# The experts' items of 128 tokens in float32 instead of split float32r, in an attention, expert and feed-forward kernel

## The chip, the core and the metric

The kernel runs on one core of a Trainium2 chip. A core has a matrix engine (TensorE, PE in the profile; its weight loads are PEld), a vector engine (VectorE, DVE), an engine for activations (ScalarE, ACT), GpSimd (POOL) and SyncE (SP), which here issues nearly all DMAs. They work side by side and wait for each other by semaphores. Operands lie in SBUF, and TensorE writes its sums to PSUM. The metric is the time of one execution on the device in microseconds (us), as the median of several runs.

## The reference

Three layers follow one another. The middle one is touched by the change: tokens that pass a skip score go to one of eight experts each, the one with the largest logit.

```python
def _moe_ref(x, w_skip, w_gate, w1, w2):      # x [4608 or fewer rows of 4352, 512], w1 [8, 512, 1024], w2 [8, 1024, 512]
    ...                                        # do_compute, e_idx, gate_w from x @ w_skip and x @ w_gate
    for e in range(E):
        mask = e_idx == e
        h = np.maximum(xc[mask] @ w1[e], 0.0)
        y[mask] = gate_w[mask, None] * (h @ w2[e])
    out[do_compute] = xc + y
```

Before it stands a two-way attention with 8 blocks of 512 + 32 rows, behind it a feed-forward layer over all 4352 rows with weights of 512 x 2048 and 2048 x 512. All arrays are float32, except those last weights, which come as float64.

## The kernel before

The program has three stages: the attention, which also routes the tokens (each token's row, its gate and its number go to a scratch array `xs`, sorted by expert); the experts (class `Experts`, method `run`); and the feed-forward layer (`ffn`, which takes up two thirds of the time).

The experts work through items. An item of 512 tokens is handled by `first` or `item_a`, one of 128 tokens by `item_b`. How many there are depends on the data; the trace shows one `first`, four rounds of the loop over `item_a` (L1037) and four of the loop over `item_b` (L1041). In these loops the item after the present one is loaded ahead: its weights come in eight DMAs of 512 KB on SP's queue, four with parts of w1 (`fetch1`, L711) into the buffers `two1` (seen by parts as `raw1`) and four with parts of w2 (`fetch2`, L717) into `two2` (`raw2`). The last round loads the weights of an item that does not exist, which nobody reads.

TensorE multiplies in float32r, a reduced form of float32. To keep the accuracy, every operand is a sum of two float32r tiles: `split` (L766 to L769) casts the raw tile on ACT (the high part) and subtracts it from the raw one on DVE or POOL (the low part). A product is then three matmuls (`PAIRS`: high x high, high x low, low x high).

An item of 128 tokens runs as follows. The rows `xb` are copied to `xc` (L983), and SP fetches the next item's rows into `xb` (L984) and its w1 (L711). Eight splits bring raw w2 to `w2p` (`split2`, the odd ones with POOL for the subtraction), each followed, after every second one, by the fetch of the next item's part of w2. `s1(0)` and `s1(1)` multiply the turned rows `xTb` by `w1p`: 24 matmuls of 512 columns (L993), and ACT applies the ReLU (L998). Then three turns by `trx` (L773 to L776: four transposes of 128 x 128 on TensorE and a split of the result): `hs[0]`, the next item's rows `xb`, `hs[1]`. `s2` multiplies the turned h by `w2p`: 24 matmuls of 512 columns (L1007); beside them the next item's w1, which has arrived, is split (`split1`). `gated` (L902) adds the result to the item's rows, `take_wait` (L906) lets POOL wait for it, and `scatter` (L732) stores the rows. The turns share two PSUM buffers (tag "tr"), so that the third has to wait until the first one's result has been split. Each engine runs its instructions in this order, and goes into the next round of the loop without a wait for the other engines.

At the end of a loop SP waits until the stores and fetches of the loop have landed (the waits of L1041), and the engines meet before the feed-forward layer begins with `fetch` of rows (L1178) and conversions of its weights (L1115 and further).

## Time and profile before

| | |
|---|---|
| median of 3 runs | 1239.1 us (1238.55 to 1243.37) |
| the profiled execution | 1242.4 us span; no time of its own around the span is given |
| TensorE busy, share of the span | 95% |
| VectorE, ScalarE, GpSimd busy | 47%, 38%, 19% |
| the rounds of `item_b`, from L993's first dense matmul to the last of L1007 | 385.88 to 459.65 us of the span |
| the first work of the feed-forward layer | 465.4 us |

Times within a trace are microseconds from the start of the span. A busy TensorE is not a TensorE at its peak: its records overlap, so the time from one start to the next (the pitch) tells its rate, not the length of a record. The granted clock (PEclk) is 1.00 at 2.4 GHz and 0.50 at 1.2 GHz; a value between is a mean over a window.

### The profile page before, as it was taken

What the parts mean: (1) busy time and instruction counts of PE and PEld (TensorE: products, weight loads), DVE (VectorE), ACT (ScalarE), POOL (GpSimd) and SP (SyncE); (2) the same over time, 40 slices, a digit from 0 to 9 for tenths busy, and PEclk for the clock granted to TensorE, in tenths of its full rate; (3) what the DMA queues carried; (4) which work ended last, traced back from release to release, by engine and by line L of the source; (5) the groups of instructions that cost most, each with busy time, mean ns of one, the idle gap of its engine ahead of it and who ended that gap; (6) DMA issues with size and microseconds to landing.
All of it is one profiled execution on the core that took longest, in us unless ns stands there. A gap on an engine that the chain in (4) does not pass through costs nothing.

```text
span 1242.4 us, 16595 instructions
## 1 busy us (share of the span) xinstructions
PE 1177.9 (95%) x5916; PEld 952.0 (77%) x5916; DVE 579.4 (47%) x993; ACT 470.2 (38%) x866; POOL 237.9 (19%) x241
## 2 busy tenths in 40 slices
PE   7898989999997768999999999999999999999998
PEld 4666767888886556888888888888888888888886
DVE  6878684535435877777432232322322322232222
ACT  7775354334335545444422222222322322222222
POOL 4666341101104545555100000000000000000000
PEclk9899989999998888999999999999999999999999
DMA  6866674524525755332210000000000000000000
GB/s 190 282 227 211 232 238 161 176 94 135 184 87 178 250 204 188 102 103 68 69 35 17 26 26 17 34 17 18 35 18 17 34 17 17 34 1 1 34 1 34
DMA packets 76048, 118.42 MB, mean 95 GB/s; under 512 B 11344, under 2 KB 48208, under 8 KB 75216
## 3 DMA queue, kind: packets, MB, share of 16 engines
q1 hardware_dynamic: 71344, 106.00, 25.7%
q0 software_dynamic: 4640, 11.57, 2.5%
q8 instruction: 40, 0.66, 0.2%
q14 instruction: 24, 0.20, 0.0%
HBM read 84.74 MB, written 36.49 MB: 98 GB/s over the span
## 4 chain that ended last, share of the span: by engine, by line
PE 52%; DVE 6%; ACT 2%; issue 2%; DMA 0%; POOL 0%; SPq 0%; DVEq 0%; ACTq 0%; POOLq 0%
PE po L1244 25%; PE ph L1224 25%; DVE gg L1231 1%; DVE cv L1122 1%; ACT g L1233 1%; PE ptx L1205 1%; DVE cv L1115 1%; DVE cv L1126 1%; DVE g L1234 1%; DVE cv L1131 1%; ACT gg L1230 1%; ACT W L1137 0%; DMA xw<-x_in_dram 0%; ACT W L1118 0%; DVE xt L1213 0%
## 5 line engine op out<-in xcount | busy, mean ns | idle before, releaser
L1244 PE MATMUL po<-W,g 128*128 128x512 f32 x1632 | 393.5, 389 | 0.0
L1224 PE MATMUL ph<-xt,W 128*128 128x512 f32 (+1 forms) x1536 | 352.5, 378 | 5.5 <-DVE gg L1231 3.3
L1244 PEld LDWEIGHTS po<-W,g 128*128 128x128 f32 x1632 | 305.3, 188 | 62.7
L1224 PEld LDWEIGHTS ph<-xt,W 128*128 128x128 f32 x1536 | 275.1, 188 | 61.2 <-DVE gg L1231 5.5
L1231 DVE SCALAR_TENSOR_TENSOR gg<-gg,ph 128x512 f32<-128x512 f32 (+1 forms) x144 | 94.8, 658 | 356.9 <-ACT gg L1230 356.9
L1230 ACT ACTIVATE gg<-ph,three 128x512 f32<-128x512 f32 (+1 forms) x144 | 95.7, 665 | 346.8 <-PE ph L1224 342.0
L1234 DVE TENSOR_TENSOR g<-gg,g 128x512 fp32r<-128x512 f32 (+1 forms) x144 | 98.9, 687 | 95.5 <-ACT g L1233 95.5
L1233 ACT CAST g<-gg 128x512 fp32r<-128x512 f32 (+1 forms) x144 | 86.1, 598 | 129.8 <-DVE gg L1231 129.8
L854 PE MATMUL ph<-xTa,w1p 128*128 128x512 f32 x480 | 120.7, 402 | 5.9 <-DVE w1p L769 4.3
L866 PE MATMUL po<-w2p,hT 128*128 128x512 f32 x480 | 120.5, 398 | 0.0
L854 PEld LDWEIGHTS ph<-xTa,w1p 128*128 128x128 f32 x480 | 91.9, 192 | 28.0 <-DVE w1p L769 4.7
L866 PEld LDWEIGHTS po<-w2p,hT 128*128 128x128 f32 x480 | 89.6, 189 | 20.1
L859 DVE SCALAR_TENSOR_TENSOR hT<-ph,hT 128x512 fp32r<-128x512 f32 x40 | 27.6, 691 | 94.3 <-ACT hT L858 91.2
L858 ACT ACTIVATE hT<-ph 128x512 fp32r<-128x512 f32 x40 | 23.9, 599 | 121.0 <-PE ph L854 121.0
L769 DVE TENSOR_TENSOR w1p<-raw,w1p 128x512 fp32r<-128x512 f32 x72 | 56.2, 805 | 9.2 <-ACT w1p L768 8.2
L769 DVE TENSOR_TENSOR w2p<-raw,w2p 128x512 fp32r<-128x512 f32 x56 | 53.7, 972 | 4.7 <-PE ph L993 4.4
L277 PE MATMUL pxr<-BD,AT 128*128 128x265 f32 x128 | 41.9, 450 | 5.0 <-ACT XR L281 1.8
L768 ACT CAST w1p<-raw 128x512 fp32r<-128x512 f32 x80 | 45.8, 620 | 2.1 <-DMA raw<-in_moe_w_dram 2.1
L1224 PE MATMUL ph<-raw,W 128*128 128x512 f32 x192 | 46.6, 391 | 0.0
L906 POOL TENSOR_TENSOR seen<-xr 128x1 f32<-128x1 f32 x24 | 8.4, 352 | 196.7 <-DVE xr L902 154.2
L1138 POOL TENSOR_TENSOR W<-cv,W 128x512 fp32r<-128x512 f32 x32 | 43.8, 1385 | 10.8 <-ACT W L1137 10.7
L768 ACT CAST w2p<-raw 128x512 fp32r<-128x512 f32 x72 | 42.3, 619 | 3.5 <-DVEq L1037 1.7
(216 smaller groups left out, 1055.3 us busy)
## 6 DMA issues: line engine op xcount, KB each, us to landing
raw<-in_moe_w_dram SPq DMA_DIRECT2D x80, 512.0 KB, 6.5
raw<-in_moe_w_in_dram SPq DMA_DIRECT2D x16, 512.0 KB
raw<-in_moe_w_out_dram SPq DMA_DIRECT2D x16, 512.0 KB
x_in_dram<-XR SPq DMA_DIRECT2D x8, 1024.0 KB
xw<-x_in_dram SPq DMA_DIRECT2D x14, 512.0 KB
out_dram<-raw SPq DMA_DIRECT2D x13, 512.0 KB
xn<-xs_dram SPq DMA_DIRECT2D x6, 1028.0 KB, 5.8
X<-in_x_dram SPq DMA_DIRECT2D x6, 1024.0 KB
```

Source lines behind the costliest of these rows:

```text
L277: nc.tensor.matmul(px, lhsT=AT[b, q][:, P * c:P * c + P], rhs=BD[:, 2 * b + q, :], start=True, stop=True,)
L768: nc.scalar.copy(hi, src)
L769: (eng or nc.vector).tensor_tensor(lo, src, hi.bitcast(F32), op=ALU.subtract)
L854: nc.tensor.matmul(ph, lhsT=w1p[a][:, f, kk, :], rhs=xTa[b][:, kk, :], start=(n == 0), stop=(n == 11))
L866: nc.tensor.matmul(po[c], lhsT=hp[f][a][:, P * c:P * c + P], rhs=w2p[b][:, f, :], start=(f == 0 and n == 0), stop=(f == NF - 1 and n == 2),)
L1138: nc.gpsimd.tensor_tensor(lo[i], a[i], hi[i].bitcast(F32), op=ALU.subtract)
L1224: nc.tensor.matmul(ph[:, :n], lhsT=W1[f][a][:, kk, :], rhs=xt[j][b][kk // 2][:, kk % 2, :n], start=(i == 0), stop=(i == 11),)
L1230: nc.scalar.activation(gg[:, :n], ph[:, :n], AF.Relu, bias=k["three"])
L1231: nc.vector.scalar_tensor_tensor(gg[:, :n], gg[:, :n], 6.0, ph[:, :n], op0=ALU.min, op1=ALU.mult)
L1233: nc.scalar.copy(hi[:, :n], gg[:, :n])
L1234: nc.vector.tensor_tensor(lo[:, :n], gg[:, :n], hi[:, :n].bitcast(F32), op=ALU.subtract)
L1244: nc.tensor.matmul(po[c0], lhsT=gg[a][:, P * c:P * c + P], rhs=W2[f][b], start=(f == 0 and i == 0), stop=(f == NFF - 1 and i == 2),)
```

## The change

`item_b` takes the raw float32 tiles as they are. The splits of w1, w2, the rows and h are gone from it, and with them the tiles `xTb` and the use of `w1p`, `w2p` and `hT`. The first product is 16 float32 matmuls of 256 columns from `two1`, the second 8 of 512 columns from `raw2`; a turn ends with one ACT copy. The next item's w1 is fetched part by part as the first product has used each part, the next w2 as the second product goes on. `first` and `item_a` stay as they are, with their splits of the next item's w1.

```diff
+        def turned32(src, dst):
+            pt = self.p_t.tile([P, 4, P], F32, tag="tr", name="ptx")
+            for j in range(4):
+                nc.tensor.transpose(pt[:, j, :], src[:, P * j:P * j + P], k["ident"])
+            nc.scalar.copy(dst, pt)
+
+        hs = [xn[:, g, 0:DM] for g in range(2)]
+        h32 = [xn[:, 2 + g, 0:DM].rearrange("p (f c) -> p f c", f=4) for g in range(2)]
+
         def item_b(i):
             en = expert_b(i + 1)
             rn = row_b(i + 1)
-            hs = [xn[:, g, 0:DM] for g in range(2)]
             xc, yb = xr[:, 0], xr[:, 1]
             nc.vector.tensor_copy(xc, xb)
             nc.sync.dma_start(xb, xs[ds(rn, P)])
-            for f in range(0, NF, 2):
-                self.fetch1(en, f)
...
+            for g in range(2):
+                ph = p_h.tile([P, 2, 2 * P], F32, tag="h", name="ph")
+                for u in range(2):
+                    for kk in range(4):
                         nc.tensor.matmul(
-                            ph, lhsT=xTb[a][:, kk, :], rhs=w1p[b][:, 4 * g:4 * g + 4, kk, :],
-                            start=(n == 0), stop=(n == 11),
+                            ph[:, u, :], lhsT=x32[:, kk, :], rhs=self.two1[2 * g + u][:, kk, :],
+                            start=(kk == 0), stop=(kk == 3),
                         )
-                        n += 1
-                nc.scalar.activation(hs[g], ph, AF.Relu)
...
+                    self.fetch1(en, 4 * g + 2 * u)
+                nc.scalar.activation(hs[g], ph.rearrange("p u f -> p (u f)"), AF.Relu)
+            nc.vector.tensor_copy(toks[:, 0:1], xc[:, DM + 1:])
+            turned32(hs[0], h32[0])
+            turned32(xb[:, 0:DM], x32)
+            turned32(hs[1], h32[1])
             po = p_o.tile([P, DM], F32, tag="o0", name="pob")
...
             for f in range(NF):
-                split2(f, nc.gpsimd if f % 2 else nc.vector)
+                nc.tensor.matmul(
+                    po, lhsT=h32[f // 4][:, f % 4, :], rhs=raw2[f], start=(f == 0), stop=(f == NF - 1)
+                )
                 if f % 2:
                     self.fetch2(en, f - 1)
...
             gated(yb[:, 0:DM], po, xc)
             take_wait(yb)
             self.scatter(yb[:, 0:DM], toks[:, 0:1])
-            for f in range(NF - 2, NF):
-                split1(f)
```

Ahead of the loop, the first item's rows are turned by `turned32(xb[:, 0:DM], x32)` in place of `trx`, and `x32` lies in the room of `xTb`.

## Rows read from the trace of the kernel before

**Rows 1.** Windows, one a round of item_b, then the loop's end; busy us (instructions), clock, DMA.

```profile
385.88:402.12 16.24, 15.16 (x60) 12.10 (x60) 9.71 (x13) 11.21 (x22) 10.70 (x9) 0.82 0.93 307
402.12:421.76 19.64, 15.62 (x62) 12.37 (x61) 16.51 (x18) 12.65 (x24) 9.65 (x8) 0.83 0.72 248
421.76:439.98 18.22, 14.26 (x62) 11.49 (x60) 15.97 (x16) 10.85 (x21) 9.69 (x8) 0.91 0.74 248
439.98:459.65 19.67, 15.31 (x61) 11.95 (x59) 16.55 (x16) 9.29 (x18) 9.66 (x8) 0.83 0.70 240
459.65:465.43 5.78, 0.16 (x1) 0.00 (x0) 1.95 (x3) 0.00 (x0) 1.56 (x2) 0.81 0.06 23
```

**Rows 2.** Groups of instructions, 385.88 to 459.65: busy us, mean ns | idle before, releaser.

```profile
L769 DVE TENSOR_TENSOR w2p<-raw,w2p 128x512 fp32r<-128x512 f32 x16 | 26.3, 1690 | 4.7 <-PE ph L993 4.4 <-ACT w2p L768 0.3
...
L769 DVE TENSOR_TENSOR w1p<-raw,w1p 128x512 fp32r<-128x512 f32 x22 | 21.7, 1027 | 0.8 <-ACT w1p L768 0.8
...
L768 ACT CAST w2p<-raw 128x512 fp32r<-128x512 f32 x31 | 16.9, 618 | 1.5 <-issue 1.5
...
L775 PE MATMUL ptx<-ident,xn 128*128 128x128 f32 x32 | 6.2, 328 | 12.9 <-DVE hT L769 12.9
```

**Rows 3.** Timeline of TensorE, first and third round: start, us, instruction [idle before].

```profile
383.49 0.79 PE L993 MATMUL ph<-w1p,xTb 128*128 128x512 f32 x1 [0.68 <-ACT xTb L768]
...
385.88 8.21 PE L993 MATMUL ph<-w1p,xTb 128*128 128x512 f32 x23 [1.60 <-issue]
...
421.76 5.74 PE L993 MATMUL ph<-w1p,xTb 128*128 128x512 f32 x24
427.33 0.60 PE L775 MATMUL ptx<-ident,xn 128*128 128x128 f32 x4
427.77 0.60 PE L775 MATMUL ptx<-ident,xb 128*128 128x128 f32 x4
432.33 0.95 PE L775 MATMUL ptx<-ident,xn 128*128 128x128 f32 x4 [3.96 <-DVE hT L769]
432.93 7.21 PE L1007 MATMUL pob<-w2p,hT 128*128 128x512 f32 x24
```

**Rows 4.** Windows of 1 us in the first and second round; clock is third from last.

```profile
390.00:391.00 1.00, 1.00 (x4) 0.81 (x3) 0.00 (x0) 0.00 (x0) 0.69 (x1) 0.50 0.83 279
391.00:392.00 1.00, 1.00 (x4) 0.76 (x4) 0.00 (x0) 0.96 (x2) 0.00 (x0) 0.70 1.12 424
...
395.00:396.00 1.00, 0.00 (x0) 0.00 (x0) 0.71 (x2) 0.75 (x2) 0.86 (x1) 1.00 1.09 360
...
412.00:413.00 1.00, 0.04 (x1) 0.05 (x1) 1.00 (x3) 0.00 (x0) 0.00 (x0) 0.54 1.07 371
...
418.00:419.00 1.00, 1.00 (x4) 0.74 (x4) 1.00 (x1) 1.00 (x3) 0.96 (x1) 0.55 1.06 410
```

**Rows 5.** Timeline, then line L277 (ns min/median/max): plain float32 matmuls in the attention.

```profile
60.79 1.06 PE L277 MATMUL pxr<-BD,AT 128*128 128x265 f32 x4
...
84.55 1.16 PE L277 MATMUL pxr<-BD,AT 128*128 128x265 f32 x4
...
L277 PE MATMUL pxr<-BD,AT x128: 387/387/810, 27.9 to 129.9; 128*128 128x265 f32 x128
```

**Rows 6.** DMA, 385.88 to 459.65: GB/s in 40 slices; weight fetches, us to landing.

```profile
GB/s 218 145 246 350 304 357 380 394 355 28 22 293 243 290 369 366 388 403 185 0 0 87 278 347 371 359 386 405 220 0 0 127 359 350 360 360 385 402 217 0
...
raw<-in_moe_w_dram SPq DMA_DIRECT2D x32, 512.0 KB, 7.5
```

**Rows 7.** Timeline, fourth round: next rows' fetch, their turn; line L692's register loads.

```profile
442.79 0.35 SPq L984 DMA_DIRECT2D xb<-xs_dram  x1
...
446.59 0.63 PE L775 MATMUL ptx<-ident,xb 128*128 128x128 f32 x4 [0.43 <-DMA xb<-xs_dram]
...
L692 SPq TENSOR_LOAD <-tab_b x9: 91/267/278, 183.3 to 434.0; - x9
```

**Rows 8.** Waits of SP's queue, 380 to 475: who for whom, us, times, longest.

```profile
SPq L1041 <- DMA x_in_dram<-xr,toks: 6.3, 1, 6.3
```

More of the change, by code (lines that the diff above doesn't have):

```diff
@@ L824, in run @@
         t = self.xp.tile([P, 2, XW], F32, tag="srows", name="xTb", bufs=1)
-        xTb = [t[:, i, 0:DM].bitcast(F32R).rearrange("p (k c) -> p k c", k=4) for i in range(2)]
+        x32 = t[:, 0, 0:DM].rearrange("p (k c) -> p k c", k=4)
         xr = None
@@ L984, in item_b @@
             nc.sync.dma_start(xb, xs[ds(rn, P)])
-            for f in range(0, NF, 2):
-                self.fetch1(en, f)
-            def s1(g):
-                ph = p_h.tile([P, 512], F32, tag="h", name="ph")
-                n = 0
-                for kk in range(4):
-                    for a, b in PAIRS:
+            for g in range(2):
+                ph = p_h.tile([P, 2, 2 * P], F32, tag="h", name="ph")
+                for u in range(2):
+                    for kk in range(4):
                         nc.tensor.matmul(
-                            ph, lhsT=xTb[a][:, kk, :], rhs=w1p[b][:, 4 * g:4 * g + 4, kk, :],
-                            start=(n == 0), stop=(n == 11),
-                        )
-                        n += 1
-                nc.scalar.activation(hs[g], ph, AF.Relu)
@@ L1000, in trh @@
-            def trh(g):
-                trx(hs[g], [t[:, 4 * g:4 * g + 4] for t in hT], slice(0, P))
-            po = p_o.tile([P, DM], F32, tag="o0", name="pob")
-            def s2(f):
-                for n, (a, b) in enumerate(PAIRS):
-                    nc.tensor.matmul(
-                        po, lhsT=hT[a][:, f, :], rhs=w2p[b][:, f, :],
-                        start=(f == 0 and n == 0), stop=(f == NF - 1 and n == 2),
-                    )
+                            ph[:, u, :], lhsT=x32[:, kk, :], rhs=self.two1[2 * g + u][:, kk, :],
@@ L1014, in item_b @@
                 if f % 2:
                     self.fetch2(en, f - 1)
-                if f == 3:
-                    s1(0)
-            s1(1)
-            trh(0)
-            trx(xb[:, 0:DM], xTb, slice(0, P))
-            trh(1)
-            nc.vector.tensor_copy(toks[:, 0:1], xc[:, DM + 1:])
-            for f in range(NF):
-                s2(f)
-                if f < NF - 2:
-                    split1(f, nc.gpsimd if f in (1, 3) else nc.vector)
             gated(yb[:, 0:DM], po, xc)
@@ L1039, in run @@
         scatter_a()
-        trx(xb[:, 0:DM], xTb, slice(0, P))
+        turned32(xb[:, 0:DM], x32)
         with tc.For_i(0, nb, 1, iteration_sync="reg_based") as i:
```

## The prediction

> **What bounds the kernel now.** I read the page first: TensorE is busy for 95% of the span, but that is mostly the feed-forward layer, which the change does not touch. So the place to look is the loop over the items of 128 tokens. Windows cut at the starts of its rounds [rows 1] give four rounds of 16.24, 19.64, 18.22 and 19.67 us, 73.8 us together, and 5.8 us behind them until the feed-forward layer starts. In the second to fourth round VectorE is busy for 16.0 to 16.6 us; TensorE's 14.3 to 15.6 us are partly at a clock below 1. The groups of instructions of the stretch [rows 2] say what VectorE does: the subtractions of the splits, at 1.0 to 1.7 us each in the mean. The timeline [rows 3] shows where that meets TensorE: the first product (24 matmuls, 5.74 us) and two turns run without a gap, then TensorE idles 3.96 us for the third turn, because the first turn's subtraction stands behind the w2 splits in VectorE's order and holds the PSUM buffer. This happens in all four rounds, 12.9 us in total (the last of [rows 2]).
>
> The idle time has a second price. In windows of 1 us [rows 4] the granted clock goes from 1.00 to 0.50 at the end of that wait (the window at 412, of the second round) and comes back only about 6.8 us later (the window at 418). Work done at 1.2 instead of 2.4 GHz takes twice as long: the second product of the third round took 7.21 us, against 5.74 for the same count of matmuls before it, 1.5 us lost [rows 3]; in the second and fourth round, with a mean clock of 0.83 instead of 0.91 [rows 1], the clock was low for 0.34 x 19.7 = 6.7 us, a loss of up to 3.4. A round is thus bound by a chain: VectorE's splits, TensorE's wait, TensorE at half clock. Transfers are not the bound: they run at 350 to 405 GB/s while a burst lasts and are near zero between bursts [rows 6].
>
> **What is removed.** Per round 16 splits of weights (16 casts of 0.62 us on ScalarE, 16 subtractions on VectorE and GpSimd) and 3 of turned tiles. All of the 12.9 us wait hangs on them. With them gone, VectorE is left with a copy, the cast of the token numbers and the gating. The splits of the first item's w1 at the end of the last item of 512 stay; nobody reads them, and they cost what they did.
>
> **What is added on TensorE.** A plain float32 matmul shows as two records: the attention calls L277 64 times (8 blocks, 4 column blocks, 2 quads), and the trace has 128 of 265 columns [rows 5]. Of these four in a row take 1.06 us, of which 0.387 is the last one's length, so the pitch is (1.06 - 0.387) / 3 = 0.224 us. A second such row has 1.16 us, pitch 0.258. I scale by columns: 0.2167 us for 256, 0.433 us for 512; by the slower row 0.249 and, with the 0.033 us as a constant, 0.466. First product: 16 matmuls, 32 records, 32 x 0.2167 = 6.9 us (8.0 by the slower row). Second product: 8 matmuls, 16 records, 16 x 0.433 = 6.9 us (7.5). I take the faster row, since 0.224 us is also close to two passes of 265 columns at 2.4 GHz (0.221), which leaves little room below (0.3 us a round); the slower row starts behind another operation, whose tail may be in it. The old products cost (5.74 - 0.39) / 23 = 0.233 us a matmul, 11.2 us for 48. So TensorE's own work grows by 2.7 us a round, against a wait of about 4 and a clock loss of 1.5 to 3.4.
>
> **The stretch between the products.** Four transposes start 0.44 us after the previous four [rows 3], so three turns take 1.3 us. The third needs the first's PSUM buffer back. Behind the last matmul of the first product stand on ScalarE the second ReLU and then the copy of the first turn, 0.6 us each like the casts of the same size [rows 2]; with a start about 0.25 us after the matmul the buffer is free at about 1.4 us, and 0.44 us later the second product starts: 1.83 us, an estimate. It cannot go under 1.3 us, and no other engine is in this chain. The first four matmuls of the second product need only the first copy, and the second copy ends under them.
>
> **The rounds.** At full clock 6.93 + 1.83 + 6.93 = 15.7 us. Rounds 2 to 4 go from 57.5 to 47.1 us, a gain of 10.4 us. The first round is worse: TensorE comes out of the wait between the loops at 0.50, does one record, stalls with "issue" and starts for good at 385.88 [rows 3], and the clock rises at about 391.6 (the window with 0.70 of [rows 4]). As the number of TensorE's instructions in a round stays the same (48 records and 12 transposes, each with a weight load, before and after), I keep that stall. Until then, at half clock (2 x 0.2167 us a record), it gets through 13 records, 14 with the first; 18 x 0.2167 = 3.9 us follow, then 1.83 and 6.93: the second product ends at 404.1 or 404.2 instead of 402.1, a loss of 2.0 us. Sum: -10.4 + 2.0 = -8.4 us.
>
> **The DMAs that move.** The fetches of w1 stood at the start of a round and now stand behind each quarter of the first product; those of w2 stood behind splits and now stand behind matmuls. SP waits for TensorE eight times in a round. Behind these waits on SP's queue stand only the other fetches, the loop's register loads and the fetch of the next rows. A part of w1 is requested when the product has used it, and needed one round less that quarter later, about 14 us; landing took 7.5 us in bursts of several [rows 6]. Eight fetches and the rows are 4.46 MB, at 370 GB/s some 12 us of a 15.7 us round. So they are hidden, and if this cover went, each us of lateness would cost a us. The tightest is the fetch of the next rows: SP can only come to it when the last fetch of w2 has been issued, at the end of the second product; ahead of it stand two register loads of 0.27 us [rows 7] with the branch and the register arithmetic of the round, 2 us together as an estimate, and the issue of that fetch. So it is issued some 2.6 us after that end, lands 3.8 us later [rows 7] at about 6.4, and is needed at 7.2 (the first product and one turn). That is 0.8 us of room. The copy L983 that frees the buffer comes at 1.3 us and is not late.
>
> **The end.** The last round fetches 2 MB that nobody reads, its last part right at the end of the second product. At the loop's end SP waits for the scatter [rows 8], and this is over within the 5.8 us behind the last product (the last of [rows 1]). A lone fetch that needs 3.8 us, as the one of the rows did [rows 7], stays under it; at the 7.5 us of the bursts [rows 6] it would add some 2. I take 0, as there is no burst here, and the 5.8 us stay. The feed-forward layer just starts earlier.
>
> The sum is -8.4 us: a span of 1234.0 in place of 1242.4, and against the median, which lies 3.3 us under the profiled span, 1239.1 - 8.4 = 1230.7 us. With the slower float32 row it would be 15.43 + 1.83 = 17.3 us a round, a gain of 5.8 in rounds 2 to 4 and a loss of 3.4 in the first: 1236.7. With 1.3 us between the products and the bare columns: 1228.
>
> **Two things that could bring the gain back.** In the new round TensorE does only transposes and short waits for 1.83 us between the products. The window at 395, in the short wait of the first round, has no work of TensorE at all and still 1.00 [rows 4]; the clock fell in the waits of about 4 us. So I take it that it holds. The other is the stall at a loop's start: 383.49 to 385.88 us in the first round, while the third round's first matmul shows no idle time before it [rows 3]. The Trainium skill (Runtime: NRT & Kernel Launch, Instruction fetch mechanics) says that a taken branch to a place outside the fetched window makes the engine wait for a transfer of its code. By that rule a body that no longer lies in the window would pay the stall in every round. The trace agrees so far, in that it shows the stall at the loop's entry alone. The body has as many TensorE instructions as before, so I take none in rounds 2 to 4.
>
> **The rivals.** (1) *The start gets better too* (0.08): no stall at 383.5, up to 2 us more: 1226.7 to 1229. (2) *The clock falls between the products* in rounds 2 to 4 as it does now: 3 x 1.5 to 3 x 3.4 us back, 4.5 to 10, so 1235.2 to 1240.9, no change. Against it speaks the window at 395; 0.09. (3) *The stall of the loop's start comes in each round*, 3 x 2.4 = 7.2 us back, 1237.9, no change; against it the third round's start; 0.04. (4) *Weights or rows come 1 to 2 us late in each round*, without the clock falling: 3 to 5 us back, 1233.7 to 1236, as the slower float32 row would give; for it speaks the room of 0.8 us, against it the idle queue; 0.14. (5) *Slower*: the next rows' fetch queues behind the w2 parts, so that the turn between the products waits. With waits like today's 4 us the clock falls as well: 4 + 3.4 us in three rounds, 22 us, 1252.9. It decides if landing takes some 8.6 us (3.8 + 0.8 + 4) instead of 3.8, a little over what the weights in bursts took [rows 6]; but ahead of the rows there is only one fetch of w2, at most two; 0.07. That the splits do not go away, or the matmuls run in one pass, the code excludes.
>
> **How the numbers follow.** The forecast has 0.58, from 1228 to 1233. A measurement here tells about 0.5% from no change, 6.2 us, so faster means below 1232.9: the forecast less a little of its upper end and rival 1, 0.63. Same: that end, rivals 2 to 4, 0.30. Slower: rival 5, 0.07. The range goes from rival 1 to rival 2, 1226.5 to 1240.5.
>
> **What would show it.** Right: rounds of 15.7 us at clock 1.00 from the second on; pitch 0.217 and 0.433 us; some 0.5 us of idle time between the products; a first round near 18 us; the feed-forward layer's start at about 457. Wrong: a TensorE wait named by the fetch of the rows or of weights, windows of 0.50 in rounds 2 to 4, or a pitch near 0.25.

## The result, and the profile after

| | before | after |
|---|---|---|
| median, side by side (us) | 1243.4 (1238.6 to 1243.6) | 1231.5 (1229.2 to 1234.1) |
| ratio, 95% interval | | 0.9908 [0.9886, 0.9929] |
| a second comparison | 1244.4 (1240.5 to 1248.1) | 1231.7 (1230.2 to 1233.4), 0.9895 [0.9872, 0.9918] |
| span of the profiled execution | 1242.4 | 1229.8 |

The kernel became faster by 11.9 us (0.9%), by 12.7 in the second comparison; the forecast was 8.4. Absolute times of the kernel before differ from one comparison to the next (1235.4 to 1244.4), so below each kernel stands against the runs of before that were made beside it.

Windows of the kernel after, cut at the first matmul of each round, then from the last product to the feed-forward layer's first turn (columns: stretch, its length; busy us and count of TensorE, its weight loads, VectorE, ScalarE, GpSimd; granted clock; DMA share; GB/s):

```profile
383.12:400.74 17.62, 17.27 (x60) 11.79 (x61) 0.74 (x2) 2.75 (x5) 3.83 (x7) 0.89 0.77 243
400.74:417.00 16.26, 15.28 (x62) 10.37 (x60) 1.33 (x3) 2.75 (x5) 1.20 (x2) 1.00 0.86 284
417.00:432.66 15.66, 15.45 (x62) 10.36 (x61) 1.33 (x3) 2.84 (x5) 1.19 (x2) 1.00 0.90 300
432.66:448.30 15.64, 15.48 (x61) 10.16 (x59) 1.33 (x3) 2.85 (x5) 1.19 (x2) 1.00 0.88 291
448.30:457.76 9.46, 0.17 (x1) 0.03 (x1) 4.00 (x7) 1.22 (x2) 2.48 (x3) 0.68 0.61 206
```

Against [rows 1]: VectorE's 16 us a round have become 1.3, the clock of rounds 2 to 4 is 1.00, and they take 16.26, 15.66 and 15.64 us. From the first product's start to the feed-forward layer's first turn it is 74.64 us (383.12 to 457.76). In the trace of before the same stretch runs from 383.49 [rows 3] to 469.07:

```profile
469.07 4.22 PE L1205 MATMUL ptx<-ident,xw 128*128 128x128 f32 x16 [9.26 <-POOL W L1133]
```

That is 85.58 us, so the loop gained 10.94: 1.01 in the first round (18.63 to 17.62), 9.97 in rounds 2 to 4 (57.53 to 47.56), nothing behind them (9.42 to 9.46). The remaining 1.7 us of the two spans lie in stages whose code the change doesn't touch, 0.4 ahead of the loop and 1.3 in the feed-forward layer. From its first turn to the end of the span the layer takes 772.0 us here, 771.9 and 772.4 in two more traces with this loop (below), and 773.3 and 774.0 in before and in the kernel with all w1 splits on VectorE; so the 1.3 us do not look like chance, but no run shows their cause.

The timeline of TensorE in the kernel after (start, us, instruction, idle before it), from the first product into the third round:

```profile
383.12 9.04 PE L999 MATMUL ph<-raw,xTb 128*128 128x256 f32 x32 [0.68 <-ACT xTb L983]
...
393.38 0.66 PE L982 MATMUL ptx<-ident,xn 128*128 128x128 f32 x4 [0.35 <-ACT xn L983]
393.87 7.03 PE L1011 MATMUL pob<-raw,xn 128*128 128x512 f32 x16
400.74 7.07 PE L999 MATMUL ph<-raw,xTb 128*128 128x256 f32 x32
407.65 0.60 PE L982 MATMUL ptx<-ident,xn 128*128 128x128 f32 x4
409.23 0.63 PE L982 MATMUL ptx<-ident,xb 128*128 128x128 f32 x4 [0.98 <-DMA xb<-xs_dram]
...
410.13 7.03 PE L1011 MATMUL pob<-raw,xn 128*128 128x512 f32 x16
417.00 7.07 PE L999 MATMUL ph<-raw,xTb 128*128 128x256 f32 x32
```

Three things are to be seen. The 32 records of the first product start 400.74 and the transposes behind them at 407.65: 0.216 us a record; the 16 of the second run from 410.13 to 417.00, 0.429 us a record. The third turn's wait of 3.96 us [rows 3] is 0.35 or less; the second turn waits 0.98 us once, for the next rows. And the first round's matmuls run from 383.12 without the stall that [rows 3] shows at 385.88; the clock is up early in it, as windows of 1 us show:

```profile
386.00:387.00 1.00, 1.00 (x4) 0.81 (x3) 0.45 (x2) 0.00 (x0) 0.82 (x3) 0.53 0.40 160
387.00:388.00 1.00, 1.00 (x6) 0.87 (x6) 0.00 (x0) 0.00 (x0) 0.50 (x1) 1.00 0.99 133
```

In before the window with the rise is the one at 391 [rows 4]. These rows are of one trace; in the second trace of this kernel (below) the first round took 18.04 us, so its gain is 0.6 to 1.0 us.

### The profile page after: what moved, and what is told of

It reads as the page before. It is cut to its first block, busy times and chain, and to the rows that moved or that the text cites. A ratio compares the mean times of both kernels' runs of the same rounds, so it can differ in the third digit from the quotient of the medians.

```text
span 1229.8 us, 16098 instructions
## 1 busy us (share of the span) xinstructions
PE 1175.9 (96%) x5916; PEld 943.8 (77%) x5916; DVE 525.3 (43%) x940; ACT 436.6 (35%) x802; POOL 203.5 (17%) x217
## 4 chain that ended last, share of the span: by engine, by line
PE 52%; DVE 6%; ACT 2%; issue 2%; DMA 0%; POOL 0%; DVEq 0%; SPq 0%; ACTq 0%; POOLq 0%
PE po L1231 26%; PE ph L1211 25%; PE ptx L1192 1%; DVE cv L1102 1%; DVE gg L1218 1%; DVE cv L1109 1%; ACT g L1220 1%; DVE cv L1113 1%; DVE g L1221 1%; DVE cv L1118 1%; ACT gg L1217 0%; ACT W L1124 0%; DMA xw<-x_in_dram 0%; ACT W L1105 0%; DVE xt L1200 0%
## 5 line engine op out<-in xcount | busy, mean ns | idle before, releaser
L277 PE MATMUL pxr<-BD,AT 128*128 128x265 f32 x128 | 40.6, 438 | 6.9 <-DVE AT L240 4.3
L1211 PEld LDWEIGHTS ph<-raw,W 128*128 128x128 f32 x192 | 35.7, 188 | 7.3
L378 POOL DMA_INDIRECT xs_dram<-XR,slot x32 | 33.5, 1046 | 33.2 <-issue 18.3
L769 DVE TENSOR_TENSOR w1p<-raw,w1p 128x512 fp32r<-128x512 f32 x48 | 33.2, 708 | 10.0 <-ACT w1p L768 8.6
L277 PEld LDWEIGHTS pxr<-BD,AT 128*128 128x128 f32 x128 | 22.2, 201 | 15.4 <-DVE AT L240 5.3
```

Of the source, the lines that this page charges most:

```text
L277: nc.tensor.matmul(px, lhsT=AT[b, q][:, P * c:P * c + P], rhs=BD[:, 2 * b + q, :], start=True, stop=True,)
L378: i = nc.gpsimd.indirect_dma_start(out=xs, out_offset=bass.IndirectOffsetOnAxis(ap=slot[:, col:col + 1], axis=0), in_=t["rows"][c], in_off ...
L769: (eng or nc.vector).tensor_tensor(lo, src, hi.bitcast(F32), op=ALU.subtract)
L1211: nc.tensor.matmul(ph[:, :n], lhsT=W1[f][a][:, kk, :], rhs=xt[j][b][kk // 2][:, kk % 2, :n], start=(i == 0), stop=(i == 11),)
```

## The experiments

**The theory.** The gain is the third turn's wait and the half clock behind it, both from the splits. Open after the result were: what the stall at the loop's entry was (code, or a wait for another engine); whether the splits cost by their amount or by their place in VectorE's order; and how near the next rows' fetch is to becoming the new wait.

### The stall at the entry: before, with the w1 splits of each round all on VectorE

```diff
-                    split1(f, nc.gpsimd if f in (1, 3) else nc.vector)
+                    split1(f)
```

> The kernel before, with the low parts of w1 in the rounds all subtracted on VectorE and none on GpSimd. Theory A: the stall of TensorE's second matmul in the first round (383.49 to 385.88 us) is a wait for GpSimd, which writes parts of w1p in the rounds and reaches the loop only when it has issued the four scatters of the last item of 512. Then the second matmul starts within 0.6 us of the first here, with GpSimd still in its scatters, while ScalarE's second cast of w2 (a tile that GpSimd still reads) stays late. Theory B: it is the code of the loop's body that has to be fetched. The body is as long as before, so the gap of about 2.4 us stays. Rounds 2 to 4 stay between 18 and 21 us by both.

Measured 1245.4 us beside 1243.4 of before, a single run. TensorE's timeline of this kernel at the entry:

```profile
382.03 7.53 PE L993 MATMUL ph<-w1p,xTb 128*128 128x512 f32 x24 [0.68 <-ACT xTb L768]
...
393.56 1.12 PE L775 MATMUL ptx<-ident,xn 128*128 128x128 f32 x4 [3.12 <-DVE hT L769]
```

All 24 matmuls run on; the stall is gone, with the loop otherwise as large as it was. So it was TensorE's wait for GpSimd, which had written parts of w1p. GpSimd's timeline of the kernel before, then the record in which its instruction queue arrives at the loop (L1041), show why that is late in the first round:

```profile
382.60 1.01 POOL L732 DMA_INDIRECT x_in_dram<-xr,toks  x1 [0.68 <-issue]
...
388.17 2.51 POOL L769 TENSOR_TENSOR w2p<-raw,w2p 128x512 fp32r<-128x512 f32 x2
```

```profile
L1041 POOLq EVENT_SEMAPHORE  x1: 17/17/17, 385.8 to 385.8; - x1
```

Ahead of the loop it runs four scatters from 382.60 on; its first split begins at 388.17. Its queue issues ahead of them and comes to the loop at 385.81, where it sets a semaphore. TensorE's second weight load, which waits for that semaphore by its own record, starts at 385.88, ScalarE's second cast, which waits for it too, at 385.86. With the w1 splits on VectorE, GpSimd's queue arrives at 384.36, ScalarE's cast still waits for it (384.41), and TensorE does not. So the code fetch of theory B is not what held TensorE. The kernel with the other order, below, has the same stall under GpSimd's name. Removing this stall alone gains nothing: the third turn then waits 3.12 us in the first round, where it waited 1.08 before.

### The wait put back: six subtractions between the two products

```diff
+        def held32(src, dst):      # turned32, with six subtractions ahead of its copy, on VectorE
...
-            turned32(hs[0], h32[0])
+            held32(hs[0], h32[0])
```

The six subtractions' results are read by nobody.

> The changed kernel, with six subtractions on VectorE (0.68 us each, results unused) ahead of the first turn's copy, which goes to VectorE too: the third turn has to wait as it did before. Theory A (the wait has a price of its own and a second one in the clock): TensorE idles about 4 us between the products, the clock falls to 0.50, and rounds 2 to 4 go from 15.7 us to 22 to 23 us, 4 of it the wait and 2 to 3.4 the second product at half clock. Theory B (the wait alone costs): 19.5 to 20 us, at clock 1.00. By A float32 with the wait is slower than the split float32r with it (18.2 to 19.7 us).

Measured 1253.5 us beside 1243.4, a single run: 22 us more than the kernel after (1231.5, beside 1243.4 as well). Its timeline of TensorE, the second round:

```profile
414.32 0.66 PE L982 MATMUL ptx<-ident,xn 128*128 128x128 f32 x4 [0.75 <-ACT xTb L983]
417.96 8.63 PE L1021 MATMUL pob<-raw,xn 128*128 128x512 f32 x16 [2.99 <-DVE xn L993]
```

The stretch between the products grows by 3.55 us (5.65 from the last record of the first product to the first of the second, against 2.1 in a round of after without a wait for rows), and the second product takes 8.63 us instead of 7.03, 10.16 in the third round; these two rounds take 20.8 and 22.3 us. It is not the third turn that waits here but the second product, for VectorE's copy. The wait came out at 3 us instead of the expected 4, and its price is of the kind that the prediction read from before: itself, and 1.6 to 3.1 us again in clock.

### Order alone: before, with the last four w2 splits behind the turns

```diff
-            for f in range(NF):
+            def w2(f):
                 split2(f, ...)          # and the fetch behind every second one
+            for f in range(4):
+                w2(f)
+            s1(0)
...                                     # s1(1) and the three turns as before
+            for f in range(4, NF):
+                w2(f)
```

> The kernel before with an order changed and no float32: the last four splits of w2 stand behind the turns instead of ahead of the first product. Theory A (the wait is one of VectorE's order, and VectorE's 16 us a round come next): the wait of 4 us shrinks to under 1.5 us, the clock stays at 1.00, and rounds 2 to 4 are bound by VectorE at 16.5 to 17.5 us; the stall at the loop's entry stays; ratio to before 0.993 to 0.997. Theory B (VectorE's sum holds TensorE wherever the splits stand): the wait moves in front of the second half of the second product, and rounds stay at 18 us and more, ratio above 0.998.

Measured 1235.9 us beside 1235.4, ratio 1.0007 [0.9986, 1.0027]: no change. TensorE's timeline, first and second round, then the window of the fourth round:

```profile
376.62 0.80 PE L993 MATMUL ph<-w1p,xTb 128*128 128x512 f32 x1 [0.68 <-ACT xTb L768]
379.02 8.04 PE L993 MATMUL ph<-w1p,xTb 128*128 128x512 f32 x23 [1.61 <-POOLq L1045]
...
398.05 7.15 PE L993 MATMUL ph<-w1p,xTb 128*128 128x512 f32 x23 [2.29 <-POOL w1p L769]
...
407.19 0.66 PE L775 MATMUL ptx<-ident,xn 128*128 128x128 f32 x4 [1.12 <-DVE hT L769]
```

```profile
430.22:447.60 17.38, 13.73 (x61) 9.98 (x60) 16.39 (x17) 11.43 (x22) 10.62 (x9) 1.00 0.81 279
```

The third turn's wait was one of order, as the prediction said: it falls from 3.9 us to 1.12 and, in rounds 3 and 4, to 0.46 and 0.76, with the clock at 1.00 there. The rounds 2 to 4 take 52.31 us, 5.2 less than in before. But they come no lower than 16.8 to 18.1 us: VectorE has 15.6 to 16.4 us of work in each, and TensorE now waits 2.3 us at the first product, for w1 parts that GpSimd, which comes to them behind its own late w2 splits, has not yet split. What the rounds gain, the stages behind them give back: VectorE starts the feed-forward layer's work 9.6 us after the last product's last record, 6.1 in before, TensorE's first turn there comes 12.5 us after the loop instead of 9.4, and the layer takes 775.0 us instead of 773.3. So under the prediction's chain lay a second bound close by, the work of VectorE and GpSimd in a round. Rounds 3 and 4 came out as in theory A, the ratio as in theory B. Here the stall at the entry is put down to GpSimd's queue by name.

### Each product alone in plain float32

First the second product alone (the first stays in float32r, its w1 low parts all on VectorE), then the first alone (w2 stays split).

```diff
+            for f in range(0, NF, 2):
+                self.fetch1(en, f)
-                            ph[:, u, :], lhsT=x32[:, kk, :], rhs=self.two1[2 * g + u][:, kk, :],
+                            ph, lhsT=xTb[a][:, kk, :], rhs=w1p[b][:, 4 * g:4 * g + 4, kk, :],
-            turned32(xb[:, 0:DM], x32)
+            trx(xb[:, 0:DM], xTb, slice(0, P))
...                                     # behind each f of the second product, as far as f < NF - 2
+                    split1(f)
```

> A part of the change alone: the second product in float32 from raw w2 and unsplit h, the first one in split float32r as before, with all low parts of w1 on VectorE. Theory A (what held TensorE was the split of w2 in front of the h splits; the splits of w1 lie beside the second product): no wait of 4 us, clock 1.00 from round 2 on, rounds of 5.6 + 1.9 + 6.9 = 14.4 to 15.5 us, no stall at the loop's entry, and a time 3 to 6 us below the changed kernel's, ratio to before 0.985 to 0.990. Theory B (all splits together held it, as VectorE's sum): VectorE is late again with the w1 splits, rounds of 17 us and more, and a ratio above 0.992.

```diff
-                    po, lhsT=h32[f // 4][:, f % 4, :], rhs=raw2[f], start=(f == 0), stop=(f == NF - 1)
+                        po, lhsT=hT[a][:, f, :], rhs=w2p[b][:, f, :],
+                split2(f, nc.gpsimd if f % 2 else nc.vector)
-            turned32(hs[0], h32[0])
+            trh(0)
```

> The other part of the change alone: the first product in float32 from raw w1 and unsplit rows, the second one in split float32r as before, with the splits of w2 (half of their low parts on GpSimd) and of h. Theory A (the splits of w2 ahead of the h splits hold the third turn): the wait stays, but is shorter, since the first product is 1.3 us longer and VectorE no longer has w1 parts ahead of its w2 parts: 1.5 to 3 us, at most a short fall of the clock, rounds of 15.5 to 17.5 us, no stall at the loop's entry, ratio to before 0.991 to 0.996. Theory B (the sum of all splits on VectorE held it): with 8 of 16 gone the wait vanishes, rounds of 14.3 us, ratio about 0.987.

The second alone: 1232.6 us beside 1243.4, ratio 0.9909 [0.9880, 0.9938]. The first alone: 1222.6 us beside 1235.4, ratio 0.9905 [0.9881, 0.9928]. Each half gives the whole gain of the change; neither gives more, as the expectations had held possible. The wait is gone in both, as theory A of the first and theory B of the second have it, but the rounds are longer than theirs, 15.7 and 15.2 us. The window of a later round of the first, then of the second of these kernels, then VectorE's w1 splits in the first:

```profile
417.93:433.67 15.74, 13.94 (x54) 8.79 (x53) 6.48 (x12) 6.16 (x11) 1.55 (x2) 1.00 0.84 275
```

```profile
408.86:424.06 15.20, 14.29 (x70) 11.76 (x69) 8.15 (x9) 7.29 (x13) 6.25 (x6) 1.00 0.87 298
```

```profile
L769 DVE TENSOR_TENSOR w1p<-raw,w1p 128x512 fp32r<-128x512 f32 x34 | 21.8, 686 | 5.7 <-ACT w1p L768 5.5
```

VectorE is at 6.5 and 8.2 us in these rounds, and no wait for it is left in TensorE's timeline between the products, though in the kernel with the first alone the w2 splits still stand ahead of the turns. (The kernel with the second alone waits for the next rows instead, 2.19, 1.80 and 1.45 us in rounds 2 to 4; the first of these lowers the clock, and that round takes 17.67 us.) Once VectorE has half of its splits it is out of the way; the other half of the change then only makes TensorE's work longer, by 0.9 us a round for either product: 24 float32r matmuls took 5.96 us in the kernel with the second product alone (400.26 to 406.22) and 6.02 in the one with the first alone (402.84 to 408.86), against 6.91 and 6.87 for the 32 and 16 plain records.

VectorE's 16 us in before are not all its own work. A subtraction takes 0.69 us in the first of these kernels, where GpSimd has none, but 1.69 in the mean for w2 in before [rows 2], where GpSimd subtracts beside it; with the w1 splits all on VectorE (the first experiment) those of w1 took 0.68 and those of w2, still beside GpSimd's, 1.94. Taking away half of the splits thus took away work and, in the first kernel, its stretching too. A kernel with all splits of before on VectorE was not run, so how much of the bound is the sum and how much the two engines side by side is not told apart.

### The next rows' fetch on ScalarE's queue

```diff
-            rn = row_b(i + 1)
+            rn = nc.scalar.value_load(tab_b[0:1, ds(1 + NB + i + 1, 1)], min_val=0, max_val=NSLOT)
-            nc.sync.dma_start(xb, xs[ds(rn, P)])
+            nc.scalar.dma_start(xb, xs[ds(rn, P)])
```

> The changed kernel, with the next rows fetched on ScalarE's DMA queue instead of SP's, where their fetch was issued 4.7 to 5.7 us after the second product's end, behind the landing of the last part of w2. Theory A: TensorE's waits for the rows (1.0 us in round 2, 0.2 us in round 3) are gone, rounds 2 to 4 are 15.6 us each, and the time falls by about 1 us, too little to be told from the changed kernel's. Theory B: the rows come late because the transfers are busy, not because of SP's order; the waits stay or grow.

Measured 1242.9 us beside 1243.4, ratio 0.9998 [0.9983, 1.0013]: the whole gain gone. TensorE's, SyncE's and ScalarE's timelines, second round:

```profile
410.22 1.09 PE L982 MATMUL ptx<-ident,xb 128*128 128x128 f32 x4 [3.79 <-DMA xb<-xs_dram]
...
411.95 9.10 PE L1011 MATMUL pob<-raw,xn 128*128 128x512 f32 x16
```

```profile
401.05 5.53 SPq L711 DMA_DIRECT2D raw<-in_moe_w_dram  x4
```

```profile
404.12 0.36 ACTq L994 DMA_DIRECT2D xb<-xs_dram  x1
```

The rows are requested at 404.12, 5.2 us after the second product's end at 398.9, as late as on SyncE; but SyncE, no longer held by them, sends w1 parts from 401.05 on. The rows land some 6 us after their request, among those parts; TensorE waits 3.79 us, and the second product takes 9.10 us instead of 7.03, its beginning at half clock. This is the prediction's rival 5, at 6.3 us in this round (21.97 against 15.66; the third took 17.42), with w1 in the place of w2.

A second form puts the same fetch one place later in the program, behind the first w1 fetch, in case the two shared a semaphore:

```diff
-            nc.scalar.dma_start(xb, xs[ds(rn, P)])
...                                     # in the loops over g and u
                     self.fetch1(en, 4 * g + 2 * u)
+                    if (g, u) == (0, 0):
+                        nc.scalar.dma_start(xb, xs[ds(rn, P)])
```

> The changed kernel with the rows' fetch on ScalarE's queue, as in the run that moved it there, but standing second instead of first among the nine fetches of a round. Theory A (the first and the ninth fetch of a round share a semaphore, so the first of a round waits until the last part of w2 has landed, on whatever queue it is): the rows are issued about 2 us after the second product's end instead of 5.2, TensorE does not wait for them, rounds 2 to 4 are 15.6 us, and SP's first fetch of w1 shows that wait. Theory B (the fetch of the rows itself depends on the parts of w2): it is issued at 5 us again, with waits of 2 to 4 us of TensorE.

Measured 1237.3 us beside 1235.4, a single run. The fetch is again requested 5.2 us after the end of the second product (398.04 after 392.86), and TensorE waits as long:

```profile
403.71 1.08 PE L982 MATMUL ptx<-ident,xb 128*128 128x128 f32 x4 [3.35 <-DMA xb<-xs_dram]
```

The second form did not part the two: by the records of the trace the rows' fetch and the last w2 part count their landings on the same semaphore in both forms, and in the kernel after, since the nine fetches of a round share eight. The queue that issues the rows waits for that semaphore. In this second form the part has landed at 397.89, ScalarE's wait ends at 397.91 and the fetch goes out at 398.04; in the first form at 403.96, 403.98 and 404.12; on SyncE, in the kernel after, at 406.28, 406.30 and 406.43. So the rows are requested late because they share a semaphore with the last w2 part, on whatever queue they are. A form in which they have one of their own was not run on ScalarE's queue.

### The kernel after again, and with its rows fetched a round ahead

The next two kernels need the first as their measure: the kernel after, unchanged.

> The changed kernel again, beside the two that follow, on one chip. By its first comparison (ratio 0.9908 [0.9886, 0.9929]) the ratio is 0.990 to 0.992, rounds 17.6, 16.3, 15.7, 15.2 us. If what the attention and the final product of the kernel gave in the first traces (about 1 to 2 us less in stages that the change doesn't touch) was chance, the ratio is nearer to 0.9915, which is 10.7 us; if the change reaches into them, it is 0.9905 or lower.

Measured 1231.7 us beside 1244.4, ratio 0.9895 [0.9872, 0.9918]. By the expectation's own rule (0.9905 or lower) the change would reach into the other stages, but the interval holds both cases. Its windows, first round and the end:

```profile
385.12:403.16 18.04, 17.69 (x61) 12.11 (x61) 0.58 (x2) 2.75 (x5) 3.85 (x7) 0.87 0.75 245
...
450.13:459.74 9.61, 0.17 (x2) 0.04 (x1) 4.03 (x7) 1.22 (x2) 2.51 (x3) 0.73 0.61 207
```

The loop takes 74.62 us (385.12 to 459.74), as in the first trace (74.64), though its rounds share it out otherwise (18.04, then 15.66, 15.65 and 15.66) and no turn waits for the rows. Ahead of the loop lie 385.12 us instead of 383.12: there alone 2 us differ from one execution to the next, more than the 1.7 us left over above.

With the rows fetched a round ahead:

```diff
-            rn = row_b(i + 1)
+            rn = self.value(tab_b, 1 + NB + i + 2, NSLOT + P)
-            nc.vector.tensor_copy(xc, xb)
-            nc.sync.dma_start(xb, xs[ds(rn, P)])
+            nc.vector.tensor_copy(xc, xd)
...
             turned32(xb[:, 0:DM], x32)
+            nc.vector.tensor_copy(xd, xb)
             turned32(hs[1], h32[1])
+            nc.sync.dma_start(xb, xs[ds(rn, P)])
```

> The changed kernel with the next rows fetched a round ahead (issued on SyncE behind the turns and kept in a second place, so that SyncE's wait for the last part of w2 lies behind it). Theory A: TensorE's waits for the rows (1.2, 2 and 1.0 us in the changed kernel) were what kept rounds two and three above the dense 15.23 us (6.69 of first product, 2.1 between, 6.44 of second): rounds two to four 15.2 each, 1.0 to 1.5 us less in all than the changed kernel. Rival B: the first product's 32 matmuls and the second's 16 are the bound and the waits for the rows lie beside the wait for the relu, so nothing changes (within 0.5 us). Rival C: the earlier fetch goes ahead of the w2 parts and makes them late: a wait for w2 of over 0.5 us in the second product.

Measured 1232.6 us beside 1244.4, ratio 0.9911 [0.9884, 0.9939]. The window of its second round, then a wait of SyncE's queue in the four rounds:

```profile
402.12:417.77 15.65, 15.30 (x61) 10.37 (x60) 1.71 (x4) 2.75 (x5) 1.47 (x2) 1.00 0.88 304
```

```profile
SPq L711 <- DMA raw<-in_moe_w_dram: 5.9, 3, 2.3
```

Rounds of 15.65 us, as in the kernel after: rival B. The 15.2 us of theory A left out one pitch of the second product's last record (0.43); 15.66 is a round without any wait for a transfer (0.35 us for ScalarE's copy is in it). The wait of 0.98 us for the rows in the first trace of after cost 0.6 us, once (16.26 against 15.66). Here the rows have a semaphore of their own, and it is the first w1 part that shares that of the last w2 part and waits for it; w1 has the time.

### The shortest round: float32r, float32 and rows ahead

The kernel with the second product alone in plain float32 waits for its rows (2.19 us in its second round), so its rows were fetched ahead too, at first on ScalarE's queue, with a row of xr as their second place.

```diff
-            xc, yb = xr[:, 0], xr[:, 1]
-            nc.vector.tensor_copy(xc, xb)
-            nc.sync.dma_start(xb, xs[ds(rn, P)])
+            xc, yb, xd = xr[:, 0], xr[:, 1], xr[:, 2]
+            nc.vector.tensor_copy(xc, xd)
...
+            nc.vector.tensor_copy(xd, xb)
             turned32(hs[1], h32[1])
+            nc.scalar.dma_start(xb, xs[ds(rn, P)])
```

> The kernel with the second product alone in float32, whose rounds lost 2.2, 1.8 and 1.5 us to the wait for the next rows. Here the rows are fetched a round earlier, on ScalarE's queue, right after the turn that frees their buffer, and kept in a second place. Theory A: these waits are gone, rounds 2 to 4 are 14.3 to 14.8 us, and the time falls by some 4 us below that kernel's and the changed one's, ratio to before 0.985 to 0.989. Theory B: the parts of w1 come late then (SP still issues them only when the last part of w2 has landed), and the rounds stay at 15.5 us or more.

Measured 1225.9 us beside 1235.4, ratio 0.9942 [0.9918, 0.9966]. Rounds 2 to 4 are 14.3 us each, without a wait for rows or weights, but the loop begins late:

```profile
380.44 8.10 PE L1004 MATMUL ph<-w1p,xTb 128*128 128x512 f32 x24 [6.85 <-ACTq L1041]
```

```profile
DVE xr L1039 <- DMA x_in_dram<-xr,toks: 4.4, 1, 4.4
```

The second fence is a wait at the entry: the copy into xr, ahead of the loop, waits for the scatter that reads this row. So the place was changed to that of the second half of h, which no scatter reads, and the fetch went to SyncE:

```diff
+        xd = xn[:, 1]
...
+            nc.sync.dma_start(xb, xs[ds(rn, P)])
```

> The first product in three float32r products with the w1 low parts all on VectorE, the second in plain float32, rows fetched a round ahead on SyncE and kept in the place of the second half of h, which no scatter reads (the earlier trial kept them in a place that the four scatters still read, and its loop began 7.9 us after the turn ahead of it). Theory A: that place was the cause of the late loop: the first product begins 1.8 us after the turn, rounds 16.3, 14.3, 14.3, 14.3; the end as there, 7.8 us to the next stage; about 4.5 us less than the changed kernel, ratio 0.986 to 0.988. Rival B: SyncE's fetch ahead of the loop, not the place, holds the loop's entry (a barrier of all engines), or the relu of the first round waits for the copy behind the first scatter: 2 to 6 us late at the first round, ratio 0.990 to 0.992.

Measured 1231.5 us beside 1244.4, ratio 0.9892 [0.9868, 0.9916], the same as the kernel after in this comparison (0.9895). Its windows of the four rounds, then two rows of TensorE's timeline:

```profile
381.29:397.31 16.02, 15.63 (x53) 10.19 (x53) 5.27 (x11) 5.75 (x11) 3.83 (x7) 0.86 0.73 240
397.31:411.63 14.32, 13.94 (x54) 8.79 (x53) 7.20 (x13) 6.69 (x13) 1.53 (x2) 1.00 0.84 298
411.63:426.58 14.95, 14.38 (x54) 8.73 (x53) 6.61 (x13) 7.22 (x13) 1.55 (x2) 1.00 0.85 296
426.58:442.26 15.68, 14.68 (x53) 8.61 (x52) 7.93 (x15) 7.81 (x14) 1.54 (x2) 1.00 0.88 314
```

```profile
381.29 7.83 PE L1002 MATMUL ph<-w1p,xTb 128*128 128x512 f32 x24 [0.68 <-ACT xTb L768]
...
430.85 2.83 PE L1002 MATMUL ph<-w1p,xTb 128*128 128x512 f32 x11 [0.50 <-DVE w1p L769]
```

The entry is in time (0.68 us), so the late loop came with the place and the queue of the first form; both were changed, and which of them it was is not told apart. The four rounds take 60.97 us, 4.0 less than the 65.01 of the kernel after beside it. But 11.46 us lie between the last product and the feed-forward layer's first turn (at 453.72), 1.85 more, and that layer takes 774.1 us to the end of the span instead of 771.9: the gain is gone again. VectorE's timeline and SyncE's waits at the loop's end in this kernel, then VectorE's timeline in the kernel after:

```profile
442.42 1.29 DVE L769 TENSOR_TENSOR w1p<-raw,w1p 128x512 fp32r<-128x512 f32 x2 [1.05 <-ACT w1p L768]
443.63 0.75 DVE L902 SCALAR_TENSOR_TENSOR xr<-pob,xr 128x512 f32<-128x512 f32 x1
```

```profile
SPq L1039 <- DMA raw<-in_moe_w_dram: 5.6, 1, 5.6
...
SPq L1039 <- DMA x_in_dram<-xr,toks: 0.2, 1, 0.2
```

```profile
450.43 0.75 DVE L902 SCALAR_TENSOR_TENSOR xr<-pob,xr 128x512 f32<-128x512 f32 x1 [10.41 <-PE pob L1011]
```

The gating starts 1.37 us after the product's end, behind the last w1 splits, instead of 0.30, and with it the scatter is late. But the last w2 part, which nobody reads, lands late too: SyncE waits 5.6 us for it instead of 3.2, and the scatter lands only 0.2 us behind it instead of 0.8. An earlier gating alone would have gained those 0.2 us. Why the transfers of this kernel end later, and the 2.2 us in the feed-forward layer, have no proven cause.

## Why the prediction came out as it did

**The rounds.** Right. 15.7 us were forecast for a round without waits, 15.66 measured, at clock 1.00. The pitches of 0.217 and 0.433 us, scaled from the faster row of [rows 5], came out as 0.216 and 0.429; the slower row was not the price. The stretch between the products was 1.83 and is 15.66 - 32 x 0.216 - 16 x 0.429 = 1.88 us. The gain of rounds 2 to 4 is 9.97 us against 10.4; the one wait for the rows (0.6 us) is more than the difference. Rival 2, a clock that falls between the products, did not come: it is 1.00 in all three.

**The first round.** Here the sum failed. The prediction kept the stall at the loop's entry, on the ground that the number of TensorE's instructions stays the same, and so let the clock rise at 391.6: a loss of 2.0 us. The stall was TensorE's wait for GpSimd's part of the w1 splits, and these are what the change removes. Without it the matmuls run from 383.12 and the clock is up at 387: a gain of 1.0 us, 3.0 better than forecast. Rival 1 had this case with 2 us and a chance of 0.08; its mechanism came true. The sign of a first round near 18 us came out too (17.62), but not for the reason given: it was counted from 385.88, behind the stall that was to stay. The row in [rows 3] names the stall "issue", which is no releaser; the w1p group of [rows 2] shows only 22 of 32 on VectorE, so that GpSimd writes the rest was there to be read. The returns to the loop's start (400.74, 417.00, 432.66) show no idle time of TensorE, so rival 3 falls. The Trainium skill (Runtime: NRT & Kernel Launch, Instruction fetch mechanics) lets a taken branch to a place outside the fetched window wait for code. Neither the entry into the changed loop nor any return in this trace shows an idle time that this would have to explain, and the stall that the prediction brought it up for was a wait for GpSimd.

**The chain of splits, wait and clock.** The wait and its price in clock were right, as the kernel with the six subtractions shows: 3.55 us of stretch, 1.6 to 3.1 us of clock in its rounds. That the third turn waits by the place of the w2 splits in VectorE's order was right as well: with the order changed its wait fell from 3.9 us to between 0.46 and 1.12. What the chain left out is how little room lay under it. With the order alone rounds 2 to 4 gained 5.2 of 9.97 us and the kernel nothing; with either half of the splits gone the kernel gained all. VectorE's 16 us a round, stretched by GpSimd's splits beside it, were the next bound. That changed no number of the forecast, as the change takes away both.

**The transfers.** Hidden, as forecast, but one term was mis-sized. The rows' fetch was to be issued 2.6 us after the second product's end and came 4.7 to 5.7 us after it (406.43 in the second round, in which the next product starts at 400.74). The waits of SyncE's queue in the kernel after say what was left out:

```profile
SPq L994 <- DMA raw<-in_moe_w_dram: 6.0, 3, 2.5
...
SPq L1028 <- DMA raw<-in_moe_w_dram: 3.2, 1, 3.2
...
SPq L1028 <- DMA x_in_dram<-xr,toks: 0.6, 1, 0.6
```

At the round's turn SyncE waited for the last w2 part to land, 2.0 us each time in the mean, since the rows' fetch shares its semaphore; the prediction let it wait for that part's issue alone. Landing then took 2.8 us where 3.8 was taken, so that of the room of 0.8 us nothing was left, and one turn waited 0.98. Rival 4 (0.14) began here and stayed small: 0.98 us once, 0.21 once.

**The end.** Right within 0.1 to the feed-forward layer's first turn: 9.42 and 9.46 us. VectorE's first work there comes at 454.5 us; 457 was the sign, and the difference is the first round's. The last fetch that nobody reads holds SyncE for 3.2 us, but the scatter lands 0.6 us after it, so it costs nothing.

**The sum.** The loop gave 10.9 us where 8.4 were forecast: 3.0 more in the first round, 0.4 less by the rows' wait. What the medians show beyond it (11.9 and 12.7) lies in stages whose code the change doesn't touch, and is not more than what two executions of the kernel after differ by ahead of the loop, 2 us. That the absolute time, 1231.5 us, came within 0.8 of the forecast 1230.7 is luck in part: the gain was 3.5 us larger than forecast, and before measured 1243.4 us beside it, 4.3 more than the 1239.1 that the forecast started from.

## What to carry to other kernels

When an engine is named as releaser by its place in a queue, add up that engine's work per round before you count on another order: if the sum is near the round, moving work moves most of the wait, and taking half of it away was here as good as taking all. A stall whose releaser the profile calls "issue" is a wait on something that is not shown; look for an engine that writes the waiting instruction's operands and is late at just that point. A fetch that is moved to an idle queue can lose its place ahead of larger transfers, and that place was worth the whole gain here. When a loop has more fetches than semaphores, look which of them share one: the later of the two waits for the landing of the earlier, on any queue.

## What the runs showed of the hardware

- A plain float32 matmul over 128 rows runs as two records of 0.216 us at 256 columns and 0.429 at 512 at full clock, 0.43 at 256 columns at the low level (383.70 to 384.56 for two, in the first round of after); a float32r matmul of 512 columns starts every 0.232 us in before (421.76 to 427.33 for 24, [rows 3]), but every 0.248 and 0.251 in the two kernels with one product in plain float32; why is open. A plain float32 product costs TensorE 14 to 24% more than the three float32r products, and needs no splits.
- Requests on two queues are not served by the need of the reader: rows of 257 KB, asked for on one queue while four weight parts of 512 KB each went out on another, landed after 6 us instead of 2.8 (404.12 to 410.22, against 406.43 to 409.23).
- A subtraction of 128x512 on VectorE takes 0.69 us when GpSimd does not subtract beside it (the kernel with the second product alone), 1.69 and 1.94 in the mean when it does (w2 in before, and with the w1 splits on VectorE).
- Rounds of 14.3 us can leave w1 too little time: in the last kernel above a split of w1 holds TensorE for 0.19 and 0.50 us in rounds 3 and 4 (14.95 and 15.68 us, DMA share 0.85 and 0.88). In the form before it, with the rows on ScalarE's queue, three rounds of 14.3 us had no such wait, so the transfers as a whole are not the bound yet.
